# A linear-attention and ReGLU block on one core: the first K weights issued earlier, and work of the first key and value groups put in another order

## The chip, the cores and the metric

The kernel runs on one core of one Trainium2 chip. The metric is the device time of one execution in microseconds (us); the profile gives one execution, from the first instruction to the last (its span). Engines are called TensorE (PE), VectorE (DVE), ScalarE (ACT), GpSimd (POOL) and SyncE (SP), whose queue issues nearly all DMAs of the part that is looked at here.

## The reference

```
x: [1, 2048, 1024] bf16; wqkv [1024, 3072], wo [1024, 1024]; W_gate, W_up [1024, 3584], W_down [3584, 1024]
phi(t) = where(t > 0, t + 1, exp(t)) + 1e-6
A(x):  q, k, v = split(x @ wqkv) in 32 heads of 32
       kv = sum_s phi(k)[s] v[s]^T ;  z = sum_s phi(k)[s]
       o  = (phi(q) @ kv) / (phi(q) . z + 1e-6)
       return o @ wo
B(x):  gate = x @ W_gate; up = x @ W_up
       return (gate * (gate > 0) * up) @ W_down
h   = x + A(layernorm(x))
out = h + B(layernorm(h))
```

## The kernel before

The program is written as one ordered list of operations for each engine; a planner adds a semaphore wait for each read or write of a buffer that another engine has used. An engine runs its list in order, so an operation that waits holds up all that stand behind it. The order in which the Python code calls things is the order of every list.

**Tokens.** The 2048 tokens are 16 tiles of 128 (st 0 to 15). A tile is loaded (`load_x1`, L644, four slots), its statistics are made, either on VectorE (`ln1_stats`, L950: two bn_stats, an aggregate, an add, and a power on GpSimd) or on ScalarE (`ln1_stats_act`, L959 and `act_stats`, L882: a mean, and a square that may be split in two halves q0 and q1, each with an accumulator, and four or five tiny GpSimd operations). ScalarE's passes write a junk result into the tile's slot of `xn`. Then `ln1_norm` (L966) writes the normalised tile on VectorE and `T1d` (L1013) has the DMA engines transpose it into `xnT`, and issues the load of the tile four later. `norm(st)` is `ln1_norm` and `T1d`. Tiles 0 and 1 are also centred and transposed on TensorE, tiles 2 and 3 on TensorE alone (`T1`).

**Products.** After eight plain pieces of V for tiles 0 to 3 (`v_piece`), keys and values are made in groups for a pair of token tiles (2p, 2p+1) by all 1024 columns. A group (`sgroup`, L1104) is a Strassen-Winograd scheme: the 2 x 2 blocks are tile by column half, the inner dimension is halved, and seven products of four matmuls (128 x 128 by 128 x 512) take the place of eight. They run in the order P1, P7, P6, P2, P5, P4, P3. The sums of token blocks Sx1 to Sx4 (`x_sums`, L1081; a list index i stands for Sx(i+1), and the first made is index 2, read by P7) and the differences of weight blocks TW1 to TW4 (`w_sums`, L1060; here called by their index, TWk0 to TWk3 and TWv0 to TWv3) are made on VectorE, in the order 2, 0, 1, 3. P7 reads Sx and TW of index 2, P6 of index 1, P5 of index 0; P4 reads TW3, P3 Sx3. TWk0 needs the first half of the K weights' first column block, `load_wkv(0, half=0)`.

Partial sums are forked with copies on ScalarE between PSUM banks a, b, c, f: after P1 `fk1` (a to b), which P6 then adds to; after P7 `s7` (f to SBUF); after P6 `fk2` (b to c), which P5 adds to; after P5 `sc` (c to SBUF), before P3 adds to c. The results: e11 from a, e22 (f + sc), e21 (b + s7), e12 (c). For keys each result goes through phi: an exp on ScalarE, then two VectorE operations, called e2 (min and add, L929) and phi (L932); e22 and e21 have a VectorE add in front (L1184). For values a result is a ScalarE copy (L1251) or a VectorE add (L1245).

Within a group there are numbered places, `hook(1)` to `hook(7)`, where first the operations in `pend[i]`, left by the group before, and then those that the caller passed are issued. hook(1) is behind fk1, hook(2) behind s7, hook(3) behind fk2, hook(4) behind P2 and e11, hook(5) behind the first step of e22, hook(6) behind P4, hook(7) at the end.

**The order of groups.** k0, v2, k1, v3, k2, v4, and so on (k with tiles 2p and 2p+1; v2 has tiles 4 and 5, v3 tiles 6 and 7). `x_sums(2)` (tiles 4, 5) is made in k0's hook 5, `x_sums(1)` in v2's hook 3, `x_sums(3)` in k1's hook 5. In v2's hook 5 stand the rest of the statistics of tile 6 (`q6b`), the squares of tile 7 (`sq`), and `norm(6)`, `norm(7)`. `kvacc(st)` (L1282) adds a tile to the KV sums in bank 0, 32 matmuls of 33 columns; it reads phi(k) in the two slots of `pk` and v. Before the change `kvaccs(0)` (tiles 0 and 1) and the mean of tile 9 stood in v2's hook 7, `kvaccs(1)` in v3's hook 6, the statistics of tile 8 in k1's hook 1. Ahead of all this the code from L2228 to L2301 issues the first loads, pieces and differences by hand.

The end of the key group's scheme, as it was:

```
            prod(c, SX(3), W(1, 1), False, "P3")
            s12 = list(e12(bank(c), B_bank[c]))
            if isphi:
                s12.pop(0)()
            ...
            pend[1] = list(s22[2:]) + s12
            if name in ("k0", "k1"):
                pend[3] = list(s21[1:])
```

Of the kernel before, what the change touches and what calls it, by code (L numbers as in the profile page):

```python
# [132 lines left out]
def bass_sequential_preLN__linear_attn_block__glu_gated_reglu__prompt_kernel(  # L133
# [71 lines left out]
    with es:  # L205
# [174 lines left out]
        def bank(b, w=512):  # L380
            return ps[:, b, 0:w]
# [273 lines left out]
        def load_wkv(nt, half=None, eng="sp"):  # L655
            for hf in ([0, 1] if half is None else [half]):
                d0 = hf * WKH
                d1 = d0 + WKH
                dma(sl_wkv[nt][hf], wkv[:, d0:d1, nt * NW:(nt + 1) * NW],
                    wqkv_v[:, d0:d1, D + nt * NW:D + (nt + 1) * NW], "ld_wkv_%d_%d" % (nt, hf),  # L660
                    writes=[B_wkv[nt][hf]], eng=eng)
# [187 lines left out]
        def ident_act(dst, src, reads, writes, name, func=ACTF.Identity):  # L849
            PL.add("act", lambda e: e.activation(out=dst, in_=src, func=func), reads=reads, writes=writes, name=name)  # L850
# [115 lines left out]
        def ln1_norm(st):  # L966
            i = st % NX1
            if st in ln1_a:
                k = ln1_a[st]
                PL.add("dve", lambda e: e.tensor_scalar(out=xn[:, st % NXN, :], in0=x1[:, i, :], scalar1=s1[:, k, 0:1],  # L970
                                                        scalar2=s1[:, k, 2:3], op0=ALU.subtract, op1=ALU.mult),
                       reads=B_x1[i] + [B_s1[k][0], B_s1[k][2]], writes=[B_xn[st % NXN]], name="ln1_%d_norm" % st)
            else:
                ln_norm_dve(ln1_k.pop(st), x1[:, i, :], B_x1[i], xn[:, st % NXN, :], B_xn[st % NXN], "ln1_%d" % st)
            if st in (2, 3):
                load_x1(st + NX1)
# [33 lines left out]
                   reads=[B_bank[b]], writes=[B_xcT[st][hf]], name="evT1c_%d_%d" % (st, hf))  # L1010
            partial.add(b)

        def T1d(st):  # L1013
            k = st % NXN
            dma_t(sl_tx[k], xnT[:, :, st * P:(st + 1) * P], xn[:, k, :], "T1d_%d" % st, reads=[B_xn[k]],
                  writes=B_xnT[st])
            if st + NX1 < NST:
                load_x1(st + NX1)

        def xnT_buf(st, dc):  # L1020
# [83 lines left out]
        def sgroup(pool, tok_major, X, SX, W, TW, e11, e12, e21, e22, name, hooks=(), isphi=True, last=False):  # L1104

            hooks = dict(hooks)

            def prod(b, x, w, start, nm):
                (xf, xr), (wf, wr) = x, w
                for kk in range(KH):  # L1110
                    xa, wa = xf(kk), wf(kk)
                    l, r = (xa, wa) if tok_major else (wa, xa)
                    o = bank(b)
                    if len(r.shape) == 3:
                        o = o.rearrange("p (a b) -> p a b", b=r.shape[2])
                    mm(o, l, r, start and kk == 0, kk == KH - 1, xr + wr, B_bank[b], name + nm, skip=True)

            def hook(i):
                for f_ in pend.pop(i, ()):
                    f_()  # L1120
                if i in hooks:
                    hooks[i]()

            a = alloc_bank(pool)
            f = alloc_bank(pool)
            b = alloc_bank(pool, True)
            prod(a, X(0, 0), W(0, 0), True, "P1")
            ident_act(bank(b), bank(a), [B_bank[a]], [B_bank[b]], name + "fk1")
            hook(1)
            prod(f, SX(2), TW(2), True, "P7")  # L1130
            grp[0] += 1
            s7, b7 = [(atmp, B_at), (btmp[:, 1, :], B_bt[1])][grp[0] % 2]
            sc, bc = btmp[:, 0, :], B_bt[0]
            ident_act(s7, bank(f), [B_bank[f]], [b7], name + "s7")
            hook(2)
            c = alloc_bank(pool, True)
            prod(b, SX(1), TW(1), False, "P6")
            ident_act(bank(c), bank(b), [B_bank[b]], [B_bank[c]], name + "fk2")
            hook(3)
            prod(a, X(1, 0), W(1, 0), False, "P2")  # L1140
            for f_ in e11(bank(a), B_bank[a]):
                f_()
            hook(4)
            prod(c, SX(0), TW(0), False, "P5")
            ident_act(sc, bank(c), [B_bank[c]], [bc], name + "sc")
            s22 = e22(bank(f), B_bank[f], sc, bc)
            if name == "v2":
                hook(5)
            s22[0]()
            if name != "v2":  # L1150
                hook(5)
            prod(b, X(1, 1), TW(3), False, "P4")
            s21 = e21(bank(b), B_bank[b], s7, b7)
            s21[0]()
            hook(6)
            for f_ in s22[1:2]:
                f_()
            prod(c, SX(3), W(1, 1), False, "P3")
            s12 = list(e12(bank(c), B_bank[c]))
            if isphi:  # L1160
                s12.pop(0)()
            if last:
                pend[1] = s12 + [s21[1]]
                return [s22[2], s21[2]]
            pend[1] = list(s22[2:]) + s12
            if name in ("k0", "k1"):
                pend[3] = list(s21[1:])
            else:
                pend[1] += list(s21[1:])
            hook(7)  # L1170

        pend = {}
# [1083 lines left out]
        for f_ in s2_[:2]:  # L2256
            f_()
        ln1_norm(1)
        T1d(1)
        load_wkv(0, half=0)  # L2260
        for f_ in s2_[2:]:
            f_()
        twk = w_sums(wkv, bw_k, tw_k, B_TWk, "TWk", KH)
# [18 lines left out]
        v_piece(2, 1, {4: lambda: T1(3), 6: m5})  # L2282
        q5()
        x_sums(0)
        twv.pop(0)()
        twk.pop(0)()
        ln1_norm(4)
        T1d(4)
        m6, q6a, q6b = ln1_stats_act(6, True)
        v_piece(3, 0)  # L2290
        m6()
        twk.pop(0)()
        ln1_norm(5)
        T1d(5)
        twk.pop(0)()
# [7 lines left out]
        def kv_hooks(p, nq):  # L2303

            sq = []
            A, B = 2 * p + 6, 2 * p + 7

            def k1():
                if p > 0 and A < NST:
                    ln1_stats(A)  # L2310
                for _ in range(nq[0]):
                    twq.pop(0)()

            def k5():
                if p < 2:
                    x_sums(p + 2)
                elif p + 2 < NP_:
                    x_sums(p + 2, 0)
                if p == 0:
                    m_, q0_, q_ = ln1_stats_act(B, True)  # L2320
                    m_()
                    sq.extend([q0_, q_])
                while p > 0 and late_q:
                    late_q.pop(0)()

            def k6():
                if p == 0:
                    twv.pop(0)()
                elif 1 < p < NP_ - 2:
                    x_sums(p + 2, 1)  # L2330
            return {1: k1, 5: k5, 6: k6}, sq
# [10 lines left out]
        def kvaccs(p):  # L2342
            kvacc(2 * p)
            kvacc(2 * p + 1)

        late_q = []
        NQ = {2: (0, 1), 3: (0, 1), 4: (0, 1), 5: (2, 2), 6: (1, 0)}
        for p in range(NP_):
            nq = NQ.get(p, (0, 0))
            hooks, sq = kv_hooks(p, nq)  # L2350
            if p == 0:
                hooks[1], hooks[3] = lambda: v_copy(b31, 3, 1), q6a
            if p == NP_ - 1:
                hooks[7] = lambda: kvaccs(NP_ - 2)
            k_group(p, hooks)
            if p + 2 < NP_:
                late = []

                def v3(p=p, sq=sq, late=late):
                    if p == 0:  # L2360
                        x_sums(1)
                        return
                    norm(2 * p + 6)
                    if 2 * p + 9 < NST:
                        m_, q0_, q_ = ln1_stats_act(2 * p + 9, True)
                        q0_()
                        late += [m_, q_]

                def v5(p=p, sq=sq, late=late):
                    if p == 0:  # L2370
                        for f_ in [q6b] + sq:
                            f_()
                        norm(6)
                        norm(7)
                        return
                    norm(2 * p + 7)
                    if late:
                        late[0]()
                        late_q.append(late[1])

                def v6(p=p, nq=nq):
                    if p > 0:
                        kvaccs(p)
                    for _ in range(nq[1]):
                        twq.pop(0)()

                def v7(p=p):
                    if p == 0:
                        kvaccs(0)
                        m_, q0_, q_ = ln1_stats_act(9, True)  # L2390
                        m_()
                        late_q.extend([q0_, q_])
                v_group(p + 2, {3: v3, 5: v5, 6: v6, 7: v7})
        assert not twq and not twv and not twk
        for i in range(ND2):
            load_wo(i)
# [272 lines left out]
```

## Time and profile before

| | |
|---|---|
| runs of the kernel before | 714.60, 714.13, 713.90 us; median 714.13 |
| the profiled execution | 714.61 us, of which the span is 712.8 us |
| TensorE clock granted | 1.00 |
| busy: PE, DVE, ACT, POOL | 706.6, 606.0, 411.5, 143.1 us |

Busy time in two stretches of 10 us around the change, as windows of the span (us):

```profile
10.00:20.00 10.00, 10.00 (x59) 4.76 (x58) 8.11 (x18) 5.79 (x11) 2.73 (x3) 1.00 1.13 330
20.00:30.00 10.00, 9.36 (x44) 3.82 (x43) 9.22 (x15) 8.57 (x19) 4.36 (x6) 1.00 0.73 197
30.00:40.00 10.00, 9.74 (x105) 3.95 (x105) 9.22 (x20) 8.95 (x20) 2.68 (x6) 1.00 0.65 228
40.00:50.00 10.00, 9.72 (x106) 4.22 (x106) 9.37 (x22) 8.46 (x18) 2.00 (x5) 1.00 0.34 80
50.00:60.00 10.00, 10.00 (x47) 4.00 (x46) 7.80 (x19) 7.69 (x15) 1.85 (x5) 1.00 0.52 105
```

After the window and its length, the columns are the busy us and number of instructions of PE, weight loads, DVE, ACT and POOL, the granted clock, the mean busy share of the 16 DMA engines and GB/s. A busy PE is not PE at its peak, since ends of matmuls are modelled; starts are what is compared. In timeline lines the first two columns are start and length in us, and the bracket gives the idle time of the engine before the line and what ended it. For a DMA the queue's line is its issue; when it landed is given in the text as issue plus time to landing.

### The profile page before, as it was taken

The numbers are of one execution on the slowest core, as the hardware profiler recorded it, in microseconds if no ns is written. First come the engines' busy times: TensorE is split into PE (matmuls) and PEld (weight loads), VectorE is DVE, ScalarE is ACT, GpSimd is POOL, SyncE is SP. The second block draws the span as 40 slices with busy tenths as digits, with TensorE's granted clock in tenths as the row PEclk, the third lists the DMA queues.
The fourth block names the chain that finished last, engine by engine and source line by source line (L and its number), as shares of the span: only waits on it lengthen the run. The fifth ranks groups of instructions, "written<-read, shape, count | busy, mean of one in ns | idle before, by whom it ended". The sixth has DMA issues, their size and how long they took to land.

```text
span 712.8 us, 13267 instructions
## 1 busy us (share of the span) xinstructions
PE 706.6 (99%) x5039; PEld 391.6 (55%) x5039; DVE 606.0 (85%) x974; ACT 411.5 (58%) x741; POOL 143.1 (20%) x206
## 2 busy tenths in 40 slices
PE   8999999999999999999999999999999999999998
PEld 3344444444444455555554658865555555547887
DVE  6988867899878899999998787888889888988985
ACT  4887666764973687878786411046666767633010
POOL 3231100114982223132312001310000000000331
PEclk9999999999999999999999999999999999999999
DMA  9843244114999799999897989995344544267996
GB/s 297 262 104 77 36 119 164 39 31 95 233 199 287 224 330 290 327 255 297 261 294 239 275 247 319 318 220 159 100 132 114 144 120 125 74 207 256 320 317 187
DMA packets 195104, 144.21 MB, mean 202 GB/s; under 512 B 53984, under 2 KB 172512, under 8 KB 195040
## 3 DMA queue, kind: packets, MB, share of 16 engines
q1 hardware_dynamic: 190048, 138.77, 66.9%
q0 software_dynamic: 4032, 3.67, 3.7%
q10 hardware_dynamic: 960, 0.92, 0.4%
q8 instruction: 40, 0.66, 0.4%
q14 instruction: 24, 0.20, 0.1%
HBM read 98.76 MB, written 32.51 MB: 184 GB/s over the span
## 4 chain that ended last, share of the span: by engine, by line
PE 93%; DMA 2%; DVE 2%; issue 1%; SPq 1%; ACT 0%
PE ps L845 93%; DMA RE<-in_A_x_dram 1%; DMA RAB<-in_A_wqkv_dram 1%; DVE RW L1068 1%; DMA RAB<-RXH 1%; DVE RC L1068 1%; SPq L637 1%; ACT RXH L885 0%; DVE RWG L1093 0%; DVE RE L1968 0%; DVE st L859 0%; DVE RX L1184 0%; DVE RE L1245 0%; DVE RWG L1908 0%; DVE RX L929 0%
## 5 line engine op out<-in xcount | busy, mean ns | idle before, releaser
L850 ACT ACTIVATE ps<-ps 128x512 f32<-128x512 f32 (+1 forms) x263 | 133.1, 517 | 182.2 <-PE ps L845 138.1
L845 PE MATMUL ps<-RC,RO 128*128 128x512 f16 x616 | 147.0, 370 | 0.0
L845 PEld LDWEIGHTS ps<-RC,RO 128*128 128x128 f16 x616 | 59.9, 98 | 53.3 <-ACT ps L850 1.2
L850 ACT ACTIVATE RE<-ps 128x512 f32<-128x512 f32 (+3 forms) x106 | 63.8, 627 | 32.1 <-PE ps L845 18.0
L845 PE MATMUL ps<-RC,RWG 128*128 128x512 f16 x320 | 81.0, 380 | 0.6 <-DVE RC L1068 0.6
L845 PE MATMUL ps<-RH,RWG 128*128 128x512 bf16 (+1 forms) x348 | 77.7, 349 | 0.0
L1977 POOL DMA_DIRECT2D out_dram<-RX x20 | 17.9, 1258 | 271.5 <-DVE RX L1968 218.4
L845 PE MATMUL ps<-RH,RO 128*128 128x512 bf16 (+1 forms) x256 | 65.3, 380 | 0.0
L1707 DVE TENSOR_TENSOR RE<-ps,RE 128x1024 bf16<-128x1024 f32 (+1 forms) x42 | 44.0, 1047 | 18.2 <-PE ps L845 18.1
L845 PE MATMUL ps<-RW,RAB 128*128 128x256 f16 (+3 forms) x374 | 56.0, 304 | 0.0
L845 PEld LDWEIGHTS ps<-RH,RWG 128*128 128x128 bf16 x348 | 33.9, 98 | 35.3 <-ACT ps L850 0.2
L845 PE MATMUL ps<-RAB 128*128 128x512 bf16 (+3 forms) x250 | 52.9, 350 | 0.0
L845 PEld LDWEIGHTS ps<-RC,RWG 128*128 128x128 bf16 (+1 forms) x320 | 29.9, 97 | 35.3 <-ACT ps L850 5.5
L845 PEld LDWEIGHTS ps<-RW,RAB 128*128 128x128 f16 (+1 forms) x374 | 36.3, 98 | 16.2 <-DVE RAB L1419 0.5
L1968 DVE TENSOR_TENSOR RE<-ps,RE 128x512 f32<-128x512 f32 x44 | 30.2, 686 | 14.4 <-PE ps L845 11.8
L1719 ACT ACTIVATE RAB<-RAB 128x1024 bf16<-128x1024 bf16 x28 | 29.5, 1053 | 18.9 <-DVE RAB L1707 18.9
L1707 DVE TENSOR_TENSOR RAB<-ps,RE 128x1024 bf16<-128x1024 f32 x28 | 34.2, 1222 | 7.2 <-PE ps L845 6.5
L1707 DVE TENSOR_TENSOR RAB<-RAB,RE 128x1024 bf16<-128x1024 bf16 x56 | 37.3, 686 | 3.1 <-ACT RE L850 2.8
L1573 DVE TENSOR_TENSOR RO<-RWG 128x1024 f16<-128x1024 bf16 x54 | 39.4, 729 | 0.0
L845 PEld LDWEIGHTS ps<-RH,RO 128*128 128x128 f16 (+1 forms) x256 | 24.3, 98 | 24.7 <-ACT RX L850 1.5
L1573 DVE TENSOR_TENSOR RO<-RWG,RO 128x1024 f16<-128x1024 bf16 x54 | 37.8, 700 | 0.0
L845 PEld LDWEIGHTS ps<-RAB 128*128 128x128 bf16 (+1 forms) x250 | 24.2, 98 | 21.8 <-ACT RAB L988 0.3
(212 smaller groups left out, 1294.0 us busy)
## 6 DMA issues: line engine op xcount, KB each, us to landing
RWG<-in_B_W_gate_dram SPq DMA_DIRECT2D x28, 512.0 KB, 6.0
RWG<-in_B_W_up_dram SPq DMA_DIRECT2D x28, 512.0 KB, 4.9
RW<-l_scr SPq DMA_DIRECT2D x20, 448.0 KB, 5.4
RW<-in_B_W_down_dram SPq DMA_DIRECT2D x14, 512.0 KB, 6.1
t_scr<-RW SPq DMA_DIRECT2D x14, 512.0 KB, 4.3
l_scr<-RX SPq DMA_DIRECT2D x7, 1024.0 KB, 8.8
RE<-l_scr SPq DMA_DIRECT2D x15, 448.0 KB, 5.4
RW<-t_scr SPq DMA_DIRECT2D x13, 448.0 KB, 5.2
```

Of the source, the lines that this page charges most:

```text
L637: return PL.add(eng, lambda e: e.dma_start(dst_ap, src_ap), reads=reads, writes=writes, slot=slot, name=name)
L845: lambda e: e.matmul(out_ap, lhsT, rhs, start=start, stop=stop, skip_group_check=skip),
L850: PL.add("act", lambda e: e.activation(out=dst, in_=src, func=func), reads=reads, writes=writes, name=name)
L1068: PL.add("dve", lambda e: e.tensor_tensor(out=t(j)(d), in0=in0(d), in1=in1(d), op=ALU.subtract), reads=reads, writes=[btw[j]], name="%s%d" ...
L1573: PL.add(eng, lambda e: e.tensor_tensor(out=tb(j, u), in0=f0(u), in1=f1(u), op=ALU.subtract), reads=[B_w[i + x] for x in r] + ([B_T[k + x] ...
L1707: PL.add("dve", lambda e: e.tensor_tensor(out=dst, in0=in0, in1=in1, op=op), reads=reads, writes=writes, name=name)
L1719: PL.add("act", lambda e: e.activation(out=d, in_=d, func=ACTF.Relu), reads=[], writes=db, name=name)
L1968: PL.add(eng, lambda e: e.tensor_tensor(out=dst, in0=in0, in1=in1, op=op), reads=reads, writes=writes, name=name)
L1977: PL.add("pool", lambda e: e.dma_start(dst, src, accum_op=ALU.add), reads=[bsrc], writes=[B_hscr[st]], slot=sl, name="acc_%d_%d" % (st, dh))
```

## The change

No operation is added or taken away; their order changes. By hand-written places:

- `load_wkv(0, half=0)` (512 KB) is issued before `T1d(1)` and the load of x tile 5 that comes with it, not after.
- TWk0 and TWk1 are made one after the other; half of TWv0 and `norm(4)` come behind.
- In k0 and k1, the exp of e22 goes to hook 1 of the next group (behind its fk1), the exp and phi of e12 to hook 3 (behind its fk2), the exp and phi of e21 to hook 5; in k0 the add of e21 goes to hook 3 too.
- In v2 and v3 the copy of e11 comes behind `sc`.
- `kvaccs(0)` goes from v2's hook 7 to k1's hook 2, `kvaccs(1)` from v3's hook 6 to k2's hook 2: between P7 and P6.
- The statistics of tile 8 go from k1's hook 1 to v3's hook 2, the mean of tile 9 from v2's hook 7 to k1's hook 5, its second half-square from k1's hook 5 to v3's hook 3; a half-square of tile 11 from v3's hook 3 to its hook 5.
- In v2, `T1d(6)` and `T1d(7)` are issued before the loads of tiles 10 and 11.

```
-        def T1d(st):
+        def T1d(st, load=True):
...
-            if st + NX1 < NST:
+            if load and st + NX1 < NST:
                 load_x1(st + NX1)
...
             prod(a, X(1, 0), W(1, 0), False, "P2")
-            for f_ in e11(bank(a), B_bank[a]):
-                f_()
+            s11 = list(e11(bank(a), B_bank[a]))
+            if name not in ("v2", "v3"):
+                run(s11, len(s11))
             hook(4)
             prod(c, SX(0), TW(0), False, "P5")
             ident_act(sc, bank(c), [B_bank[c]], [bc], name + "sc")
+            run(s11, len(s11))
             s22 = e22(bank(f), B_bank[f], sc, bc)
...
             s21 = e21(bank(b), B_bank[b], s7, b7)
-            s21[0]()
+            if name != "k0":
+                s21[0]()
             hook(6)
-            for f_ in s22[1:2]:
+            for f_ in s22[1:1 if name in ("k0", "k1") else 2]:
                 f_()
             prod(c, SX(3), W(1, 1), False, "P3")
             s12 = list(e12(bank(c), B_bank[c]))
-            if isphi:
+            if isphi and name not in ("k0", "k1"):
                 s12.pop(0)()
...
-            pend[1] = list(s22[2:]) + s12
-            if name in ("k0", "k1"):
-                pend[3] = list(s21[1:])
-            else:
-                pend[1] += list(s21[1:])
+            pend[1] = list(s22[1 if name in ("k0", "k1") else 2:])
+            (pend.setdefault(3, []) if name in ("k0", "k1") else pend[1]).extend(s12)
+            if name == "k0":
+                pend[3].append(s21[0])
+            (pend.setdefault(5, []) if name in ("k0", "k1") else pend[1]).extend(s21[1:])
...
         ln1_norm(1)
+        load_wkv(0, half=0)
         T1d(1)
-        load_wkv(0, half=0)
...
         x_sums(0)
-        twv.pop(0)()
+        twk.pop(0)()
         twk.pop(0)()
         ln1_norm(4)
         T1d(4)
         m6, q6a, q6b = ln1_stats_act(6, True)
         v_piece(3, 0)
         m6()
-        twk.pop(0)()
+        twv.pop(0)()
...
             def k1():
-                if p > 0 and A < NST:
+                if p > 1 and A < NST:
                     ln1_stats(A)
...
-                while p > 0 and late_q:
+                while p == 1 and m9:
+                    m9.pop(0)()
+                while p > 0 and len(late_q) > (p == 1):
                     late_q.pop(0)()
...
+            if p in (1, 2):
+                hooks[2] = lambda p=p: kvaccs(p - 1)
             k_group(p, hooks)
...
+                    if p == 1:
+                        late_q.pop(0)()
                     norm(2 * p + 6)
                     if 2 * p + 9 < NST:
                         m_, q0_, q_ = ln1_stats_act(2 * p + 9, True)
-                        q0_()
                         late += [m_, q_]
+                        if p == 1:
+                            late.append(q0_)
+                        else:
+                            q0_()
...
                         for f_ in [q6b] + sq:
                             f_()
-                        norm(6)
-                        norm(7)
+                        ln1_norm(6)
+                        T1d(6, False)
+                        ln1_norm(7)
+                        T1d(7, False)
+                        load_x1(6 + NX1)
+                        load_x1(7 + NX1)
                         return
                     norm(2 * p + 7)
+                    for f_ in late[2:]:
+                        f_()
...
                 def v6(p=p, nq=nq):
-                    if p > 0:
+                    if p > 1:
                         kvaccs(p)
...
                     if p == 0:
-                        kvaccs(0)
                         m_, q0_, q_ = ln1_stats_act(9, True)
-                        m_()
+                        m9.append(m_)
                         late_q.extend([q0_, q_])
...
+                if p == 1:
+                    vh_[2] = lambda: ln1_stats(8)
```

## The prediction, made before the changed kernel was run

> **What bounds the kernel now.** I read the waits of TensorE first, over the whole span (columns: us in total, times, longest):
>
> ```profile
> PE ps L845 <- POOL RXH L618: 1.4, 1, 1.4
> PE ps L845 <- DVE RC L1068: 0.6, 1, 0.6
> PE ps L845 <- DVE RWG L1093: 0.3, 1, 0.3
> PE ps L845 <- ACT ps L850: 0.3, 1, 0.3
> ```
>
> TensorE is the bound (706.6 of 712.8 us busy). Its own waits are small and all lie early. The chain of waits says where the unbroken work starts:
>
> ```profile
> 38.25 0.55 DVE RXH L970
> ...
> 39.70 3.77 DMA RAB<-RXH
> ...
> 43.49 0.44 DVE RWG L1093
> ...
> 43.98 629.05 PE ps L845 x4441
> ```
>
> From 43.98 us on TensorE runs 629 us without a gap, so what counts is when the product that starts there, P7 of v3, can start. The chain behind it: tile 7's normalisation at 38.25, its transpose T1d(7), the sum Sx2 made from it. TensorE's timeline shows the stalls ahead:
>
> ```profile
> 23.06 1.02 PE L845 MATMUL ps<-RC,RWG 128*128 128x512 f16 x4
> 24.73 1.02 PE L845 MATMUL ps<-RC,RWG 128*128 128x512 f16 x4 [0.64 <-DVE RC L1068]
> ...
> 31.25 1.04 PE L845 MATMUL ps<-RW,RWG 128*128 128x512 f16 x4 [0.26 <-ACT ps L850]
> ...
> 43.98 1.91 PE L845 MATMUL ps<-RW,RWG 128*128 128x512 f16 x8 [0.28 <-DVE RWG L1093]
> ```
>
> A product of four matmuls takes 0.865 start to start where nothing stalls (62.10, 62.97, 63.83). From P7 of k0 (23.06) to P7 of v3 there are 21 products and one KV sum of 64 matmuls (35.76 to 36.40, 0.64): 18.8 us, so 41.86; it is 43.98. The 2.1 us between are all that can be won here: 0.81 before P6 of k0 (TWk1 late), 0.44 before P6 of v2 (copy fk1 late), 0.43 before P7 of v3, 0.16 before P6 of k1, the rest in gaps of 0.03 to 0.05 before P5 and P3, which every later group has too.
>
> **Part 1: first K weights and the order of TWk.** VectorE ended x_sums(0) by 20.41, ran half of TWv0, then stood 0.67 us until the weights' half (0,0) landed, and ran TWk0 at 21.76, norm(4), TWk1 at 23.36 (ends 24.58, P6 at 24.73). Now TWk0 and TWk1 follow each other: ready 2.6 after TWk0's start. With the weights there, that is long before P6's turn (23.92), and the copy fk1 (23.39 to 23.97) sets P6 at 24.0: up to 0.73 won. TWv0's half and norm(4) go behind; TWv1 still follows it, and no product reads either before P6 of v2 (31.25).
>
> What it costs lies on SP's queue:
>
> ```profile
> 12.42 0.49 SPq L637 DMA_DIRECT2D RE<-in_A_x_dram  x1
> 12.96 2.02 SPq L641 DMA_TRANSPOSE RAB<-RXH  x1
> 15.03 0.58 SPq L637 DMA_DIRECT2D RE<-in_A_x_dram  x1
> 15.65 0.43 SPq L637 DMA_DIRECT2D RAB<-in_A_wqkv_dram  x1
> ```
>
> The 512 KB now go ahead of T1d(1) and the load of x tile 5. The DMA engines are full then (share 0.98 to 1.31 from 12 to 20 us). By issue plus time to landing, everything lands in the order of issue: wkv3's halves at 9.9 and 11.3, T1d(0) 15.96, x4 16.6, T1d(1) 17.66, x5 18.3, weights 21.74, x6 22.3. Half a weight block costs the one behind it 1.4 (9.9 to 11.3). So T1d(1) lands at 19.05, x5 at 19.7, the weights near 18 (20 with the lag seen below). x_sums(0) starts at 19.1 and not 18.81; TWk0 at 20.7. More important is ScalarE, whose mean of tile 5 reads x5:
>
> ```profile
> 19.05 1.06 ACT L885 ACTIVATE RXH<-RE 128x1024 bf16<-128x1024 bf16 x1
> ...
> 22.34 1.06 ACT L885 ACTIVATE RXH<-RE 128x1024 bf16<-128x1024 bf16 x1
> ...
> 23.39 0.58 ACT L850 ACTIVATE ps<-ps 128x512 f32<-128x512 f32 x1
> ```
>
> From 19.05 to past fk1 ScalarE has no idle time, so a mean at 19.75 puts fk1 0.7 later, 24.09 to 24.67, and P6 at 24.72. I take this: nothing won at P6. Ends: x5 not later, P6 24.0 (0.73 won); x5 later by 2.1 more, P6 26.8 (2.1 lost). That 2.1 is a row: the weights landed 3.44 behind x5, the next such half 1.3 behind x6, so one slow DMA engine held a landing back by 2.1.
>
> [...]
>
> **Part 2: exps behind the forks.** In v2, ScalarE's order was:
>
> ```profile
> 29.59 0.63 ACT L925 ACTIVATE RX<-RX 128x512 bf16<-128x512 f32 x1 [0.41 <-DVE RX L1184]
> 30.13 0.58 ACT L925 ACTIVATE RX<-ps 128x512 bf16<-128x512 f32 x1
> 30.61 0.59 ACT L850 ACTIVATE ps<-ps 128x512 f32<-128x512 f32 x1
> ```
>
> Two exps of k0, one waiting for VectorE's add, stood before fk1. With them behind, fk1 runs when P1 of v2 is done (start 29.08, plus 0.87, plus the 0.26 that copies follow the next product's start): 30.21 to 30.79. P7 then waits for Sx2 of x_sums(2). VectorE's row, by start-to-start steps: norm(5) 24.65 (its statistics are 0.7 late through ScalarE, on GpSimd 2.15 from accumulator to result as before), TWk3 +0.46, TWv0's half +1.14, TWv1 +0.72, e2 +1.14, phi +0.32, add +0.61, Sx2 +0.60 = 29.64; P7 0.48 later at 30.12 (29.95 before), P6 30.98 (31.25). Won so far: 0.27.
>
> **Part 3: what waits for the deferred work.** k0's add of s21 and its exp now come in v2, ahead of the squares of tiles 6 and 7 on ScalarE. VectorE: Sx2 29.64, TWv3 +1.58 = 31.22, e2 +1.14, phi +0.32, e2 +0.61, phi +0.32, add +0.61 = 34.22, done 34.90. ScalarE's exp 34.93, square of tile 6 +0.54, first half-square of tile 7 +0.61, second +0.74 = 36.82 (35.99 before). From there to norm(7) took 2.26 (38.25 - 35.99): now 39.08, 0.83 later. But T1d(7) stood behind T1d(6) and the load of x10 until 39.70; with both loads behind it, it issues at norm(7)'s end, 39.68: the same. Its landing is the gain: 3.7 and 3.8 where an x load was issued just ahead (25.39, 39.70), 2.7 where none was (23.48, 37.74), 3.3 to 4.5 later in the run. I take 3.2, as T1d(6) is near: 42.88. Sx2 and P7 +0.5: **43.4**, against 43.98. Ends of this term: 42.9 (2.7) to 44.7 (4.5).
>
> TensorE's own arrival: P6 of v2 30.98, P3 after sc 34.5, k1's P1 35.4, P7 36.2, KV sums 37.1. Their second half reads phi of s21, done 37.4; all of TensorE stands behind it, but the first half (0.32) covers that. P6's turn is 37.75; fk1 of k1, behind the second half-square, ends at 38.0: 0.3 lost, 0.9 without the KV sums as cover. P2, P5, P4, P3 and v3's P1 follow (ScalarE's sc holds P5 and P3 by 0.05 to 0.1): P7's turn is 43.3. So it and Sx2 come together.
>
> **Part 4: at no cost.** The statistics of tile 8 (four VectorE operations, 39.91 to 41.54) leave the stretch before x_sums(3) and stand in v3; norm(8) follows at 48.4 (48.47 before) and x_sums(4), at 55.81 before, has its transposes by 54.9, P7 of v4 wanting them at 56: 1 us of cover, its loss comes 1:1 on the path beyond that. The mean of tile 9 (1.04 at 36.62, before fk1) goes behind sc of k1, where ScalarE had idle time; GpSimd's small operations of both go along, and its queue was idle 3.3 and 5.4 us before them. x10 and x11 load 1 to 2 us later; first read at 50.58, 7 us of cover. The KV sums keep their 128 matmuls for each pair.
>
> **The sum.** 0.58 of 712.8. The profiled execution took 714.61, 1.81 around its span; the median is 714.13, 0.48 below it. Forecast 714.13 - 0.58 = **713.5**. About 0.2% (1.4 us) can be told from no change here.
>
> **Rivals.** (1) x5 is not late: P6 of k0 at 24.0, all of v2 0.7 earlier, norm(7) at 38.4, T1d(7) at 39.0, landing 42.2, P7 of v3 42.65: 712.8. For it: the queue stood 2.02 in T1d(1)'s issue, and the weights may go while it fills. Against: full engines. (2) T1d(7) takes 3.8 as before: 43.48 landed, P7 43.98: the stalls only move, 714.1. (3) **Slower**: a slow DMA engine holds x5 to 21.8, through the mean of tile 5 P6 of k0 starts at 26.8; TensorE's row from there to P7 of v3 is 20 products, a KV sum and some 0.2 of small gaps, 18.1, so 44.9: 715.1. It decides from x5 landing after 20.8 (P6 25.85, plus 18.1 = 43.95). For it: the lag of 2.1 did occur between 18.3 and 21.7; against: it need not hit x5.
>
> **How the numbers follow.** Forecast 0.45 (own range 712.9 to 714.2), (1) 0.27, (2) 0.13, (3) 0.15. Range 712.4 to 715.1: from (1) with the landing of 2.7 to (3). Faster by over 0.2% (under 712.7) wants nearly all of the 2.1: 0.25, most of (1) and an edge of the forecast. Slower (over 715.56): 0.12, x5 past 22.2 or a missed cover in part 4. Same: 0.63.
>
> **What would show it.** x5 landing near 19.7 and the mean of tile 5 idle on a DMA until then (part 1); fk1 of v2 before its exps near 30.2; T1d(7) issued near 39.7 with no load ahead; P7 of v3 near 43.4; no gaps behind. Wrong it would be with a P6 of k0 after 25.9, or a new gap between 44 and 60.

## The result, and the profile after

The changed kernel takes 715.61 us (median of 21 runs, 714.16 and more), the kernel before 714.49 in the same rounds (21 runs): a ratio of 1.0015, 95% interval 1.0008 to 1.0022. Measured twice more it stood at 1.0021 (1.0011 to 1.0030) and 1.0020 (1.0011 to 1.0029). Two of the 21 runs had a granted clock of 0.75 and 0.56 and took 921 and 1239 us; the ratio is that of the others. The first ratio is under the 0.2% that the prediction set as what can be told from no change, the other two are at it; all three intervals lie above 1. The forecast was 713.5: the gain that it counted came, and was more than lost again 13 us later.

The trace of after is of an execution of 714.91 us, below that kernel's median; a later trace, called the third here, is of one of 715.62 and so the typical one. Waits of TensorE, after:

```profile
PE ps L845 <- POOL RXH L618: 1.4, 1, 1.4
PE ps L845 <- DVE RWG L1093: 0.9, 2, 0.4
PE ps L845 <- ACT ps L850: 0.6, 1, 0.6
```

The wait for TWk1 (DVE RC) is gone, a wait for a copy stands in its place, and the wait for VectorE's token sums (RWG) has grown from 0.3 to 0.9, now two waits. TensorE's timeline of after says where:

```profile
24.76 1.04 PE L845 MATMUL ps<-RC,RWG 128*128 128x512 f16 x4 [0.56 <-ACT ps L850]
...
30.00 1.93 PE L845 MATMUL ps<-RW,RWG 128*128 128x512 f16 x8
...
43.20 1.89 PE L845 MATMUL ps<-RW,RWG 128*128 128x512 f16 x8
...
55.21 1.03 PE L845 MATMUL ps<-RAB 128*128 128x512 bf16 x4
56.65 1.04 PE L845 MATMUL ps<-RW,RWG 128*128 128x512 f16 x4 [0.41 <-DVE RWG L1093]
58.13 1.02 PE L845 MATMUL ps<-RW,RWG 128*128 128x512 f16 x4 [0.45 <-DVE RWG L1093]
59.00 1.03 PE L845 MATMUL ps<-RAB 128*128 128x512 bf16 x4
```

The last four are P1, P7, P6 and P2 of v4. The same four in TensorE's timeline of the kernel before, P7 and P6 in one line:

```profile
56.10 1.03 PE L845 MATMUL ps<-RAB 128*128 128x512 bf16 x4
56.96 1.93 PE L845 MATMUL ps<-RW,RWG 128*128 128x512 f16 x8
58.73 1.03 PE L845 MATMUL ps<-RAB 128*128 128x512 bf16 x4
```

P6 of k0 starts at 24.76 (24.73 before), P7 and P6 of v2 follow each other, P7 of v3 starts at 43.20 in place of 43.98: 0.78 won. Then P7 of v4 starts 1.44 behind P1 and P6 1.48 behind P7, where a product takes 0.865: 1.19 lost. P2 of v4 starts at 59.00, 0.27 later than before (58.73); the 0.14 missing in this sum are smaller gaps on the way, which are fewer after. The third trace has the same with more of it:

```profile
57.45 1.04 PE L845 MATMUL ps<-RW,RWG 128*128 128x512 f16 x4 [1.02 <-DVE RWG L1093]
58.93 1.02 PE L845 MATMUL ps<-RW,RWG 128*128 128x512 f16 x4 [0.44 <-DVE RWG L1093]
59.79 1.03 PE L845 MATMUL ps<-RAB 128*128 128x512 bf16 x4
```

P2 of v4 at 59.79 is 1.06 later than before; the medians differ by 1.1 to 1.4. From P2 of v4 to the end of the span before took 654.07, after 654.10, the third trace 654.11: all of the difference lies ahead of 60 us. The chain of waits of after, at the same place:

```profile
38.56 0.55 DVE RXH L970
39.13 3.03 DMA RAB<-RXH
42.19 0.44 DVE RWG L1093
...
50.02 0.54 DVE RXH L970
50.59 5.56 DMA RAB<-RXH
56.17 0.42 DVE RWG L1093
56.59 0.60 DVE RX L1187
...
58.13 615.17 PE ps L845 x4316
```

Read from the end: the unbroken run of TensorE now starts at P6 of v4 and not at P7 of v3. It waited for VectorE's sums of tiles 8 and 9, these for the transpose of tile 9, T1d(9), which took 5.56 us from issue to landing. In the kernel before it was issued at 51.04 and landed 3.3 later, at 54.38 (the queue's line, and the DMA view at that moment):

```profile
51.04 1.23 SPq L641 DMA_TRANSPOSE RAB<-RXH  x1
...
RAB<-RXH SPq DMA_TRANSPOSE x1, 3.3
```

The queue after:

```profile
48.60 1.23 SPq L641 DMA_TRANSPOSE RAB<-RXH  x1
49.89 0.57 SPq L637 DMA_DIRECT2D RE<-in_A_x_dram  x1
50.59 1.24 SPq L641 DMA_TRANSPOSE RAB<-RXH  x1
51.93 0.52 SPq L637 DMA_DIRECT2D RE<-in_A_x_dram  x1
```

The same four issues stand in the same order in the kernel before: T1d(8), the load x12, T1d(9), the load x13. T1d(8) landed after 2.7 us (3.5 before), x12 after 5.2 (2.9), x13 after 4.9 (2.8). So it isn't the transpose alone that is slow: all that was in the DMA engines at that time is.

What else was there, the DMA views of short windows show. First 53 to 54 us of after, then 54 to 55 (the row of tenths is the mean busy share of the 16 engines; under it packets, and per queue packets, MB and share):

```profile
DMA  9090200200900000000000000000000000000000
...
q1 hardware_dynamic: 10, 0.01, 38.4%
q8 instruction: 1, 0.02, 5.8%
...
DMA packets 33, 0.01 MB, mean 8 GB/s; under 512 B 33, under 2 KB 33, under 8 KB 33
```

A queue called instruction moved one packet of 16 KB, on one DMA engine (5.8% of 16 engines' microsecond, 0.93 us of one). Then for a microsecond 33 packets of 256 B trickle. T1d(9) is 1,024 such packets in this trace: 505 start from 52.2 to 53.1 (20 of these take 1.95 to 2.31 us), the 33 from 54.1 to 55.0, and 486 from 55.0 to 55.5. In the kernel before the same packet fell in 49 to 50 us, where the engines had nothing else to do at that moment:

```profile
DMA  0000000000000000000000000000090000000000
...
DMA packets 1, 0.02 MB, mean 16 GB/s; under 512 B 0, under 2 KB 0, under 8 KB 0
...
q8 instruction: 1, 0.02, 5.5%
```

Even there T1d(8), whose data came just behind it, took 3.5; in after, with no such packet near it, it took 2.7.

There are 40 of these packets in the span (q8 instruction: 40, 0.66 MB). TensorE's 5,039 matmuls and 5,039 weight loads, 10,078, make 252 for each of the 40. From this count, and from the queue's name, I take them for fetches of TensorE's instructions; that is an estimate, as no view names the engine that they are for. No wait of TensorE is put down to one here. T1d(9), with one in its flight, took 1.3 to 2.7 us longer in the runs below.

The change put the KV sums of tiles 2 and 3, a burst of 64 matmuls and 64 weight loads, from v3 into k2, that is from 48.41 to 50.25 us. In the kernel before the fetch came 1.3 behind the burst's start.

### The profile page after: what moved, and what is told of

It reads as the page before. It is cut to its first block, busy times and chain, and to the rows that moved or that the text cites. A ratio compares the mean times of both kernels' runs of the same rounds, so it can differ in the third digit from the quotient of the medians.

```text
span 713.1 us, 13262 instructions
## 1 busy us (share of the span) xinstructions
PE 707.2 (99%) x5039; PEld 392.8 (55%) x5039; DVE 606.4 (85%) x974; ACT 411.5 (58%) x741; POOL 141.6 (20%) x206
## 4 chain that ended last, share of the span: by engine, by line
PE 92%; DMA 3%; DVE 1%; issue 1%; ACT 1%; SPq 0%; POOL 0%; DVEq 0%; POOLq 0%
PE ps L845 92%; DMA RAB<-RXH 2%; DMA RE<-in_A_x_dram 1%; ACT RXH L885 1%; SPq L637 0%; DVE RWG L1093 0%; DVE RE L1971 0%; DVE st L859 0%; DVE RXH L970 0%; ACT RE L1057 0%; DVE RWG L1911 0%; DVE RE L1248 0%; DVE RX L1187 0%; ACT RX L850 0%; POOL s L909 0%
```

## The experiments

**Theory A**: the moved KV burst moves the fetch into the flight of x12 and T1d(9), they land late, and P7 and P6 of v4 wait. **Theory B**: it is the later norm(9) (50.02 against 49.53) and the load x12 ahead of T1d(9), and the fetch only happens to be there. **Theory C**: part 1 (the weights ahead) costs it in the first 25 us.

### Undoing one part of the change

The changed kernel unchanged, first again (a_same); then with the second burst back in v3 (a_kv1); with part 1 undone (a_wkv); and with nine idle matmuls at the start cut into 24 narrower ones, so that TensorE's instructions count 30 more (a_dum):

```
a_kv1:  hook 2 of k2: no kvaccs(1);  hook 6 of v3:
-                    if p > 1:
+                    if p > 0:
                         kvaccs(p)
a_wkv:
-        load_wkv(0, half=0)
         T1d(1)
+        load_wkv(0, half=0)
         ...
-        twk.pop(0)()
+        twv.pop(0)()
         twk.pop(0)()
         ...
-        twv.pop(0)()
+        twk.pop(0)()
a_dum:
-        pe_dummies(9, [KVB] + P1_POOL)
+        pe_dummies(24, [KVB] + P1_POOL, 192)
```

> The changed kernel as it is, for a second trace of it. In the first trace P7 of v3 started at 43.20 us (43.98 before), and v4 then lost 0.57 before its P7 and 0.61 before its P6, because T1d(9) landed 5.6 us after its issue (3.3 before). Theory 1 (the late landing belongs to the new order): P7 of v3 near 43.2 again, T1d(9) landing 5 or more after its issue, the same two gaps in v4, time 1.0 to 1.4 above the kernel before. Theory 2 (a DMA engine lags now here, now there): P7 of v3 near 43.2, but T1d(9) landing 3 to 4 after its issue and no gap in v4, or a gap at another place.

> The changed kernel, with the KV sums of tiles 2 and 3 back in hook 6 of v3, ahead of k2. Theory 1a (the KV sums, moved to behind P7 of k2, put an instruction fetch of TensorE into T1d(9)): no fetch on the DMA engines between the issue and the landing of T1d(9), landing within 3.5 of issue, no gap before P7 and P6 of v4, time 1.0 or more below the changed kernel. Theory 1b (T1d(9) is late for another reason of the new order, such as its issue 0.5 earlier behind the x load): gaps in v4 as in the changed kernel, time within 0.3 of it.

> The changed kernel with part 1 undone: the first K weights behind T1d(1) and x5, and TWk0, TWk1 in their old places. If the early weights cost (x5 late, ScalarE 0.7 late) without giving anything back: P6 of k0 near 24.7 as in both kernels, the mean of tile 5 near 19.05 and not 20.03, P7 of v3 within 0.3 of 43.2, time within 0.3 of the changed kernel. If part 1 is the loss of 1.1: time within 0.3 of the kernel before.

> The changed kernel with the 9 idle matmuls at the start (512 columns) cut into 24 of 192 columns: the same columns, but 30 more TensorE instructions, so every later instruction fetch falls 30 instructions, about 3 us, earlier against the work. Theory 1a (a fetch inside T1d(9)): the fetch of 53.0 goes to about 50, T1d(9) lands within 3.7 of its issue, no gaps in v4, time 0.8 to 1.2 below the changed kernel. Theory 1b or 2: gaps and time as in the changed kernel, within 0.3.

Medians: 715.68, 716.55, 714.89 and 717.87, beside 714.25 for the kernel before.

**a_same** bears out its theory 1: T1d(9) took 5.6 and P7 and P6 of v4 waited 0.77 and 0.45, at a ratio of 1.0021. (A stall of 2.08 at 8.56 us shifts all its later times, so P7 of v3 starts at 45.86.)

**a_kv1 missed.** The burst came back, but in v3 it now waits for phi(k), which the change has deferred to k2. TensorE's timeline of a_kv1:

```profile
48.54 0.28 PE L845 MATMUL ps<-RE 128*32 128x33 bf16 x16 [0.53 <-DVE RE L932]
50.52 0.42 PE L845 MATMUL ps<-RE 128*32 128x33 bf16 x32 [1.70 <-DVE RE L932]
```

And two windows of it (behind the busy times of the five engines stand the granted clock, the DMA share and GB/s):

```profile
50.00:52.00 2.00, 1.15 (x34) 0.74 (x36) 2.00 (x4) 0.41 (x2) 0.58 (x1) 0.62 0.85 155
52.00:54.00 2.00, 2.00 (x6) 0.74 (x5) 1.07 (x4) 0.00 (x0) 0.72 (x2) 0.53 2.16 172
```

The burst ended at 50.9, as late as in the changed kernel, the fetch fell at 53.3, T1d(9) took 6.0, and TensorE stood 2.2 us and then had a clock of 0.62 and 0.53. The move of the sums can't be undone without the deferral: this run says what it saves, not what it costs.

**a_wkv**: 0.8 below a_same and 0.6 above the kernel before, so it meets neither of its two forecasts. In its trace P6 of k0 starts at 24.63, P7 of v3 at 43.62, T1d(9) takes 5.9, and P7 of v4 waits 1.09. So the loss in v4 is there without part 1.

**a_dum** missed too. The fetch by T1d(9) stayed in its flight (at 55.9, 2.4 behind the burst's start), T1d(9) took 5.3, and P7 and P6 of v4 waited 0.50 and 0.44; why 30 instructions more didn't bring this fetch forward, the runs don't show. But the first fetch moved from 19.2 in after to 17.3, into the first K weights, T1d(1) and x5: from issue to landing these took 6.7, 7.2 and 5.9 in place of 5.1, 5.6 and 4.4. x5 landed at 21.11, and ScalarE's copy was late, in TensorE's timeline of a_dum:

```profile
25.92 1.04 PE L845 MATMUL ps<-RC,RWG 128*128 128x512 f16 x4 [1.98 <-ACT ps L850]
```

This shows the effect of a fetch at another place: all that was changed is how the idle matmuls at the start are divided, and three transfers in flight land 1.5 to 1.6 late.

### The fetch elsewhere, and the loads elsewhere

In b_kvh5 the second burst goes further back, behind P5 of k2 (its KV sums take phi of half of tile 4 for that of tile 2 there, so what it computes is no longer the block, and only its times are of use). In b_t89 the loads x12 and x13 are issued behind T1d(9). b_p1 is the kernel before with part 1 alone. b_first is the changed kernel with the work on k1 and v3 put back as it was, but for the place of the statistics of tile 8: only part 1, k0, v2 and their deferrals are left.

```
b_kvh5:  hooks[5] of k2 = its own operations, then kvaccs(1);  hook 2 without it
b_t89:   in v3's hooks 3 and 5
-                    norm(2 * p + 6)
+                    ln1_norm(8)
+                    T1d(8, False)
...
-                    norm(2 * p + 7)
+                    ln1_norm(9)
+                    T1d(9, False)
+                    load_x1(8 + NX1)
+                    load_x1(9 + NX1)
b_p1:    the kernel before, with the lines of a_wkv the other way round
b_first: v3's copy of e11 before sc; k1's exp of e22, its e12 and e21 as before; kvaccs(1) in v3's
         hook 6; ln1_stats(8) in v3's hook 3, behind fk2
```

> The changed kernel with the KV sums of tiles 2 and 3 later still: in hook 5 of k2, behind P5, not behind P7. In five traces of the new order T1d(9) landed 5.3 to 6.0 after its issue (3.3 before) with an instruction fetch of TensorE in between, and the fetch came 0.4 to 3 us after the burst of 128 KV matmuls. Theory A (the burst calls for the fetch, the fetch holds one DMA engine): the fetch comes after T1d(9)'s data, T1d(9) lands within 4 of its issue, no gap before P7 and P6 of v4; P6 of k2 loses its cover, 0.6 to 0.7; time 0.3 to 0.7 below the changed kernel. Theory B (the transpose is slow for its place behind the load of x12, whatever TensorE fetches): landing 5 or more, gaps as before, time 0 to 0.7 above the changed kernel.

> The changed kernel with the loads of x12 and x13 behind T1d(9), as it does for tiles 6 and 7. Theory A (fetch): T1d(9) still lands 4.5 or more after its issue, gaps in v4 remain in part (0.5 to 1.2 in sum), time within 0.5 of the changed kernel. Theory B (x12 ahead of it): landing 2.7 to 3.8, no gaps, time 0.9 to 1.2 below the changed kernel.

> The kernel before with part 1 alone: first K weights ahead of T1d(1) and x5, TWk0 and TWk1 together. By the prediction: x5 lands near 19.9 and not 18.3, the mean of tile 5 near 20.0, P6 of k0 near 24.75 (24.73 before), so nothing won: time within 0.3 of the kernel before. Rival (part 1 costs by itself, as its undoing lowered the median by 0.8): time 0.5 to 1.0 above the kernel before. Other rival (x5 not late): 0.5 to 0.7 below.

> The changed kernel with all that concerns k1 and v3 put back (exps of k1, copy in v3, KV sums of tiles 2 and 3 in hook 6 of v3), but the statistics of tile 8 in hook 3 of v3, behind k1's phi. If the loss sits in the second group alone: P7 of v3 near 43.2, T1d(9) landing within 4 of its issue, no gap in v4, time 0.5 to 0.8 below the kernel before. If T1d(9) is again hit, or the KV sums wait for k1's phi on VectorE: gaps of 0.5 or more between 47 and 58, time as the changed kernel.

Medians: 715.47, 714.07, 714.65 and 715.14, beside 714.26 for the kernel before.

**b_kvh5**: x12 stands ahead of T1d(9) as in the changed kernel, norm(9) is later still (T1d(9) issued at 51.24), but the fetch falls at 56.5, behind both. T1d(9) landed 3.4 after its issue, x12 3.0, and no sum is late in v4. The DMA view at T1d(9)'s issue, and that of 56 to 57 us:

```profile
RAB<-RXH SPq DMA_TRANSPOSE x1, 3.4
...
q8 instruction: 1, 0.02, 5.5%
```

The load ahead doesn't do it alone. (The burst itself waits 0.88 for phi there, and P6 of k2 0.51 for a copy: at 1.0022, 1.0014 to 1.0031, the time is no better than the changed kernel's, against the 0.3 to 0.7 expected.)

**b_t89**: here the order of TensorE stays, and the load goes. The fetch falls into the gap between the data of T1d(8) and of T1d(9), at 51.4; T1d(9) took 3.5, and no gap follows. That is what was written for B (2.7 to 3.8) and not for A (4.5 or more). With b_kvh5, which has the load ahead and no delay, it says that the changed kernel needs both: the load x12, with which the fetch comes 3.0 behind the burst's start and not 1.2 as here, and the fetch. The time is that of before, ratio 0.9998 (0.9989 to 1.0007), where the changed kernel stands at 1.0015 to 1.0021: 1.2 to 1.6 us regained.

**b_p1**: 1.0008 (0.9999 to 1.0017). x5 landed at 19.85 and P6 of k0 started at 24.65, waiting 0.47 for ScalarE's copy: as expected to the tenth, nothing won.

**b_first**: 1.0015 (1.0006 to 1.0023). P7 of v3 at 43.19, as in after; but its P6 then waits 0.50 for the copy that k1's exps now stand in front of, and P6 of v4 0.45, because T1d(9) was issued at 52.74. It landed 3.6 later, with the fetch at 49.8. So this mixture isn't a better kernel, against what was expected. As it also makes the statistics of tile 8 later, and with them T1d(8) and T1d(9), it doesn't show what k1's deferrals are worth by themselves.

### One part alone, the repair again, and the repair without part 1

```
c_bkv:   the kernel before, plus
+            if p == 2:
+                hooks[2] = lambda: kvaccs(1)
...
-                    if p > 0:
+                    if p > 1:
                         kvaccs(p)
c_t89:   b_t89 again
c_t89w:  b_t89 with part 1 undone as in a_wkv
c_after: the changed kernel again
```

> The kernel before with one part alone: the KV sums of tiles 2 and 3 move from behind P5 of v3 to k2's hook 2, behind P7 of k2; everything else as before. Theory (the burst of 128 TensorE instructions calls TensorE's instruction fetch while x12 and T1d(9) are in the DMA queues): the fetch moves from 49.7 us to between 52 and 54, T1d(9) lands 5.0 to 6.0 us after its issue in place of 3.3, and P7 of v4 waits 0.3 to 1.1 us for VectorE's sums of tile 4 (its predecessor in P6's place by 0.4); time 0.3 to 1.3 above before, 714.6 to 715.6. Rival A (lateness of norm(9) in the changed kernel, 0.5 us, and the loads ahead of it make the gap, the fetch only shifts): T1d(9) lands 3.3 to 3.7 after its issue, no gap in v4, time within 0.3 of before. Rival B (the move of the burst gains, P6 of v3 starting 0.3 earlier): 713.9 to 714.1.

> The changed kernel with the loads x12 and x13 behind T1d(9), a second time and on the chip of the version that follows. Theory: T1d(9) lands 3.3 to 3.7 us after its issue, no gap at v4's P7 and P6, 713.7 to 714.3, so at 0.997 to 1.000 of before and 1.2 to 1.8 below the changed kernel. Rival (the first measurement was a lucky placement of the fetch, which a second trace would put into T1d(9) again): T1d(9) 5.0 or more after its issue and 715.0 to 715.8.

> The same with part 1 undone (first K weights back behind T1d(1) and the V weights). If the two edits add (part 1 undone was worth 0 to 0.8 in the changed kernel): 713.3 to 714.0, P7 of v3 at 43.1 to 43.7, no gap at v4's P7. Rival (part 1 shifts only the point at which the fetch falls, and without it the fetch falls into T1d(9) or T1d(8) again): a landing of 5 us or more in one of the two, 714.5 to 715.5.

> The changed kernel itself once more, on the chip of the three others, for the differences. Theory: the fetch falls between 52 and 55 us, T1d(9) lands 5.0 to 6.0 us after its issue, gaps of 0.4 to 0.8 at v4's P7 and 0.4 at its P6, 715.2 to 715.8. Rival (the late T1d(9) was an accident of two profiled executions): 3.3 to 3.9 after its issue, no gap, and the loss of 1.1 to 1.4 somewhere else in the trace.

Medians: 714.88, 713.90, 713.86 and 715.65, beside 714.23 for the kernel before. The third trace shown above is c_after's: the fetch at 54.0, T1d(9) at 5.8 and the time came as expected, and the wait before P7 of v4 (1.02) is longer than the 0.4 to 0.8 written.

**c_bkv** is half a hit. From the kernel before, moving the burst alone takes the fetch from 49.7 to 53.6, and T1d(9) from 3.3 to 5.1. The DMA view of c_bkv at the moment of T1d(9)'s issue:

```profile
RAB<-RXH SPq DMA_TRANSPOSE x1, 5.1
```

The landing of T1d(9) stands in this trace in sixteen parts. Fifteen came by 54.20, 3.6 after its issue, and the last at 55.67: one part alone holds the transfer back by 1.5.

And TensorE's timeline of c_bkv:

```profile
51.14 0.71 PE L845 MATMUL ps<-RE 128*32 128x33 bf16 x64
...
57.07 1.93 PE L845 MATMUL ps<-RW,RWG 128*128 128x512 f16 x8
```

But no gap follows, against what I had written: VectorE began the sums at 55.91, and TensorE, which is 0.9 us later in k2 than in after (burst at 51.14 against 50.25), reached P7 of v4 at 57.07. It takes both: a late T1d(9), and a TensorE that has won time ahead of it. Its ratio, 1.0008 (0.9999 to 1.0017), decides nothing by itself.

**c_t89** repeats b_t89: P7 and P6 of v4 without a gap, 0.9995 (0.9986 to 1.0004), 1.75 below c_after on the same chip. T1d(9) took 3.8, a little above what I wrote. TensorE's timeline of c_t89:

```profile
55.28 1.03 PE L845 MATMUL ps<-RAB 128*128 128x512 bf16 x4
56.14 1.94 PE L845 MATMUL ps<-RW,RWG 128*128 128x512 f16 x8
57.91 1.03 PE L845 MATMUL ps<-RAB 128*128 128x512 bf16 x4
```

And its DMA view from 51 to 52 us:

```profile
DMA  9999986321000000000000000900000000000000
...
q8 instruction: 1, 0.02, 7.7%
```

The engines are empty from 51.25 on but for the fetch, and P2 of v4 starts at 57.91: 0.82 ahead of the kernel before, the whole gain of P7 of v3 (43.25 against 43.98, 0.73) kept.

**c_t89w** is 1.8 below the changed kernel and 0.4 below the kernel before; its ratio to that, 0.9989 (0.9981 to 0.9998), only just excludes 1. Its trace is of its fastest execution, 712.79: the first fetch ran at 19.0 (19.5 in a_wkv, 19.7 in the kernel before), the first K weights landed at 19.93 (21.64 and 21.74 there), and P6 of k0 didn't wait. The medians of c_t89w and c_t89 are 0.04 apart, so part 1 neither pays nor costs there; the 0.8 that a_wkv gained over a_same was not seen again.

All traces in one table (us; the times of T1d(9) and x12 are from issue to landing; the fetch is the one nearest to T1d(9), with what the engines had to do when it started):

| kernel | KV burst starts | fetch | x12 | T1d(9) | P2 of v4 |
|---|---|---|---|---|---|
| before | 48.41 | 49.7, engines empty | 2.9 | 3.3 | 58.73 |
| b_p1 | 48.20 | 49.8, in T1d(8) | 4.0 | 3.7 | 58.53 |
| b_first | 48.28 | 49.8, engines empty | 3.1 | 3.6 | 59.22 |
| after | 50.25 | 53.3, in x12 and T1d(9) | 5.2 | 5.6 | 59.00 |
| c_after | 50.43 | 54.0, same | 5.5 | 5.8 | 59.79 |
| a_wkv | 50.68 | 54.4, same | 5.5 | 5.9 | 60.10 |
| c_bkv | 51.14 | 53.6, in T1d(9) | 3.1 | 5.1 | 58.84 |
| b_kvh5 | 54.79 | 56.5, behind them | 3.0 | 3.4 | 59.80 |
| b_t89 | 50.18 | 51.4, engines empty | behind | 3.5 | 57.78 |
| c_t89 | 50.31 | 51.6, engines empty | behind | 3.8 | 57.91 |
| c_t89w | 49.37 | 50.7, engines empty | behind | 3.8 | 56.97 |

a_same, a_kv1 and a_dum, whose earlier stalls shift all later times, have the fetch in the flight of both too, and T1d(9) at 5.6, 6.0 and 5.3. In all seven traces with the fetch in T1d(9)'s packets it took 5.1 to 6.0, in the seven without it 3.3 to 3.8. (T1d(8) in after, with neither load nor fetch near it, took 2.7. So the 3.5 to 3.8 of b_t89, c_t89 and c_t89w, with no load ahead, still hold some delay behind the fetch just before.) **Theory A** holds as to the fetch: c_bkv brings it in, b_kvh5 takes it out, and T1d(9) follows; a gap needs the addition from c_bkv. **B** falls as the whole cause by b_kvh5, but its load has a part, as b_t89 shows; its late norm falls because T1d(9) was issued 0.45 earlier than before in after and 0.07 later in c_after (50.59 and 51.11 against 51.04, where the queue had held it). **C** falls by a_wkv's trace, which has the loss in v4 without part 1, and by c_t89 and c_t89w, 0.04 apart with and without it.

Open is why, with a fetch that keeps one engine busy for 0.9 to 1.4 us (2.4 in a_same), a landing comes up to 2.7 later. In the seven traces with a quick T1d(9) it ran 1.2 to 1.7 behind the burst's start; in after, c_after and a_wkv, with x12's packets ahead, 3.0 to 3.7, in c_bkv 2.5, but in a_same 1.2. It may be queued behind them on its engine, and packets of T1d(9) behind it, but that was not shown: no view has the order within one engine. Nor is it one part alone every time: in after one of x12's sixteen parts came at 53.69 and the other fifteen only at 55.06 to 55.11.

## Why the prediction was wrong

**What counts** (the start of P7 of v3, since no gap followed): right for the kernel before, and it no longer held after. The chain of after starts at P6 of v4.

**Part 1** (x5 19.7, mean of tile 5 19.75, P6 of k0 24.72, nothing won): 19.96, 20.03, 24.76, and P6 waited for ScalarE's copy as the text has it. Right, and the rival with x5 not late (712.8) fell.

**Part 2** (P7 of v2 at 30.12, P6 without a wait): 30.00, no wait. Right.

**Part 3** (norm(7) 39.08, T1d(7) landing 3.2 after its issue, P7 of v3 43.4, with TensorE's turn at 43.3): norm(7) 38.56, landed 42.16 (3.0 after its issue), P7 43.20 with no wait, at TensorE's turn. The gain was 0.78 and not 0.58; the rival in which T1d(7) takes 3.8 fell. In c_after the landing, 42.86, fits the forecast's 42.88 by luck: T1d(7) was issued at 40.04 and not 39.68, and took 2.8 and not 3.2.

**Part 4, "at no cost", is the step that failed.** It had two terms. "x_sums(4), at 55.81 before, has its transposes by 54.9, P7 of v4 wanting them at 56: 1 us of cover": P7's turn was 56.1 as written, but T1d(9) landed at 56.15, and at 56.9 in the typical execution. All of that is its latency: the text gives T1d(9) none of its own, the rows that it names for later transposes run from 3.3 to 4.5, and it measured 5.6 and 5.8. It was issued at 50.59 in after, 0.45 earlier than before, though norm(9) ended later. The second term gave the KV sums no price because "The KV sums keep their 128 matmuls for each pair". (By the timeline they are 64 matmuls, x64, with 64 weight loads.) Their number doesn't change; but with their place the fetch moves (in c_bkv, where they alone were moved, from 49.7 to 53.6), and the term left that out. The stall grew as the text gave it, 1:1 beyond the cover: in c_after Sx2 begins at 56.96 where P7's turn was 56.26, and 0.7 of lateness and 0.5 of VectorE's own sum make the 1.19 by which P7 is late.

**The sum**: -0.58 forecast; measured ahead of v4 -0.62 in c_after (43.36 against 43.98), then +1.68 (16.43 from P7 of v3 to P2 of v4 against 14.75) gives +1.06, against the medians' 1.1 to 1.4. The slower rival had the wrong place (x5, P6 of k0) but the right kind of cause: no run shows a "slow DMA engine" apart from a fetch, and its lag of 2.1 in the kernel before is that of one part (fifteen of the sixteen of the first K weights landed by 19.75, the last at 21.74) and lies where a fetch lies (19.7 us; with the fetch at 19.0 in c_t89w they landed at 19.93, at 20.3 in c_bkv at 20.85). "A new gap between 44 and 60" was named as what would make the prediction wrong, and it is there.

## What to carry to other kernels

When a burst of small instructions is moved along TensorE's order, ask where the next packet of the instruction queue goes: here there were 40 of 16 KB for 10,078 matmuls and weight loads, and with one in its flight T1d(9) landed 1.3 to 2.7 us later than without. Keep a load that isn't urgent out of the way of a transfer that is: issuing x12 and x13 behind T1d(9) gave 1.2 to 1.75 us back. And a gain ahead of a transfer uses up that transfer's cover, so the cover has to be worked out at the new time, with the worst latency and not the usual one.

## What was not expected of the hardware

In three traces a stall of TensorE was followed by a lower granted clock. In a_dum the wait of 1.98 before P6 of k0 was followed by a granted clock of 0.75 and 0.50, means over its windows of 2 us:

```profile
26.00:28.00 2.00, 2.00 (x8) 0.85 (x9) 1.97 (x4) 1.81 (x4) 0.05 (x1) 0.75 0.76 158
28.00:30.00 2.00, 2.00 (x6) 0.63 (x5) 1.80 (x3) 0.86 (x3) 0.00 (x0) 0.50 0.99 246
```

Over 27.0 to 30.4 us alone the clock is 0.50, and 1.00 on both sides. The products from P2 on take 1.50, 1.70 and 1.07 from start to start in place of 0.865, 1.7 us more on top of the stall. After a wait of 2.08 that ended at 8.56 us in a_same the means were 0.62 and 0.53 (0.50 from 8.5 to 11.9), after the 1.70 of a_kv1 the same (0.50 from 50.5 to 53.9); after waits of 1.02 (c_after) and 1.09 (a_wkv) it stayed at 1.00. The 1.70 stood in a stretch with 0.53 of another wait.
